# A three-stage kernel (DFT, dense layer, mixture of experts): paced scatters, ScalarE's copies ahead of Gelu, another table of modes, two small products moved

## The chip, the core and the metric

The kernel runs on one core of a Trainium2 chip. The metric is the device time of one execution in microseconds; shown are the median of three runs and one profiled execution. The engines are TensorE (PE; its weight loads are PEld), VectorE (DVE), ScalarE (ACT), GpSimd (POOL) and SyncE (SP, which only starts transfers). Each works through its own queue in order and waits on semaphores of the others.

## What is computed

The reference takes x of 8 batches x 3072 positions x 256 features and does this:

```python
X = np.fft.fft(np.fft.fft(x, axis=1), axis=2).real       # (8, 3072, 256)
x = X.reshape(8 * 3072, 256)
h = x @ w_in                                             # 256 -> 2048
x = (h * (1.0 / (1.0 + np.exp(-1.702 * h)))) @ w_out     # 2048 -> 256
logits = x @ w_gate                                      # 8 experts
expert_idx = np.argmax(logits, axis=1)                   # each expert takes its
# first `capacity` tokens (768), in order of position; for those
out[i] = gate_w[i] * (relu(x[i] @ w1[e]) @ w2[e])        # all others stay 0
```

## The kernel before

The second DFT, over features, is folded into w_in, so the kernel keeps matrices G = DFT x w_in in two parts (a high part in TensorE's 32-bit format and the rest), and the first DFT runs as products of fp16 halves with tables (fft_mm). The symmetry of a real input's transform lets each batch be computed for 1537 rows alone.

The middle part (phase2) goes over 8 batches of 64 units each, 512 units. A batch has four blocks of 384 rows, a block 16 units, one unit per 128 of the 2048 hidden features. In unit u TensorE makes pe, the cosine sum of unit u+1 (m1_even), and po, the sine sum of unit u (m1_odd). E is pe brought out of PSUM. It has two modes, chosen by a table of 64 digits (MODES; the first and last batch have tables of their own): in mode 1 VectorE brings it out and adds a product of two vectors (line 761), in mode 2 TensorE adds that product as a fourth matmul (line 756) and ScalarE copies (line 759). E has three buffers, pe two. VectorE then makes h = E + po and E - po (lines 774, 775), ScalarE the Gelu of h (line 787), and every fourth unit TensorE multiplies the Gelus of four units into acc (line 796), the logits.

Beside these units other work is put in by a timetable: lists pre and post for each unit, worked off ahead of and behind the unit's own operations. It holds, for the next batch, the folds of x on POOL (lines 391 to 408), the scale of that batch (fft_scale: maxima, two small products on TensorE into a tile pss, a few one-column operations on VectorE), the split into fp16 halves, the DFT products, and the preparation of the next block (m1_prep: transpositions psuv, a broadcast psb, u). The tuple SCALE says at which units of a batch the steps of fft_scale run, a negative number meaning ahead of the unit. The tiles pss, psuv, psb and others share one bank of PSUM, so each waits until the one before has been read out.

It also holds the routing of the batch before (route): the logits are transposed, the place of each token in its expert's list is worked out on VectorE, which ends in the addresses ad (line 914), and 24 scatters on POOL (line 920) write 128 rows of 48 bytes each into a table in DRAM, one scatter per unit in the code's order. POOL's queue has no other order than that of the code, and a scatter waits for nothing of its unit. The table is read in the third part (phase3), which gathers each expert's rows, runs the dense layer again for them and then the expert.

Batches count from 0 in the code; the text counts them from the first. The routing of the sixth batch (b = 5 = B - 3) runs within the seventh.

Of the kernel before, what the change touches and what calls it, by code (L numbers as in the profile page):

```python
# [10 lines left out]
F32 = mybir.dt.float32  # L11
# [12 lines left out]
B, S, D = 8, 3072, 256  # L24
# [18 lines left out]
LOADAT = (1, 3, 8)  # L43
NU, CONV, OWN, START1, START = 64, 10, 18, 26, 0
PREP = (5, 8, -9, 10, -11, 12, -13, -14)
SCALE = (-4, 5, -6, 7, -8, 8, 9)
FSTEPS, SSTEPS, SPLIT, SSPAN, SSPAN1 = 20, 9, 13, 11, 10
POINTS = ((16, -11), (25, 5), (29, 13))
SPLIT1, BETWEEN, LAST = 11, 17, (32, 41, 50)
PART = [0, -1, 1, 1, 1, 2, 2, 4, -5, 5, 5, 5, 6, 6, 6, 7, 7, 7, 7, 8, 8, 8, 9, 9, 9]  # L50
ROUTE = [2, -3, 3, -4, 4, -5, 5, 6, 7, 8, 9, 17, -18] + list(range(18, 63))
MODES = [int(c) for c in "1111111212111121122221221111111211111111111111121111111111111121"]
MODES0 = [int(c) for c in "2112111111222122211211221222211212122211222222121112111121112112"]
MODES7 = [int(c) for c in "1111111222212221211222222222112221222122212222222122121212222212"]
ORDER = ((0, 0), (1, 0), (2, 0), (2, 1), (0, 1), (1, 1), (2, 2), (0, 2), (1, 2))
# [126 lines left out]
class K:  # L182
# [561 lines left out]
    def m1_even(self, b, i, f):  # L744
# [4 lines left out]
        x = self.uvt[b, i]  # L749
        mode = (MODES0 if b == 0 else MODES7 if b == B - 1 else MODES)[NFC * i + f]  # L750
        fs = slice(f * P, (f + 1) * P)
# [192 lines left out]
    def timetable(self):  # L944
# [10 lines left out]
        def steps(gen, u0, units):  # L955
            for u in units:
                (pre if u < 0 else post)[u0 + abs(u)].append(gen)
# [28 lines left out]
        for b in range(1, B):  # L986
            s, e = start[b], NU * b
            steps(self.fft_scale(b), s, SCALE)
            s += SPLIT if b > 1 else SPLIT1
# [18 lines left out]
    def route(self, b, parts):  # L1008
        for tiles, t0, nt in parts:
            for a in tiles:  # L1010
                yield from self.route_tiles(b, *a, wait=nt != 15)
                yield
            if b < B - 1:
                del self.lt[b]
            yield from self.route_pos(b, t0, nt)
            for c in range(nt):
                self.route_scatter(b, t0, c)
                yield
            del self.addr[b, t0]
# [8 lines left out]
    def phase2(self):  # L1028
        nc = self.nc
        self.lt, self.info, self.addr = {}, {}, {}  # L1030
        self.hn = 0
        blocks = [(b, i) for b in range(B) for i in range(4)]

        self.parts = [[([(0, 3, 0)], 0, 3)], [([(3, 3, 0)], 3, 3)], [([(6, 3, 0)], 6, 3)],
                      [([(9, 3, 0), (0, 4, 1), (4, 4, 1), (8, 4, 1)], 9, 15)]]
        self.whole = [([(0, 4), (4, 4), (8, 4)], 0, 24)]
        gs, pend, after = {}, [], []
        clears = self.clears()
        hprev, evens = None, []
        accs = {}  # L1040

        def flush_logits():
            j, q, tiles = pend.pop(0)
            b, i = blocks[j]
            if q == 0:
                accs[j] = self.bank("acc", "acc")
            self.m1_logits(b, i, q, tiles, accs[j])
            if q == NFC // 2 - 1:
                after.append((b, i, accs.pop(j)))

        def evac():
            while after:
                b, i, acc = after.pop(0)
                self.m1_evac(b, i, acc)

        def gelu(hp):
            j, f, h = hp
            gs.setdefault((j, f // 2), []).append(self.m1_gelu(*blocks[j], f, h))
            if f % 2 == 1:
                pend.append((j, f // 2, gs.pop((j, f // 2))))  # L1060

        pre, post = self.timetable()

        def take(todo):
            while todo:
                next(todo.pop(0), None)

        for j, (b, i) in enumerate(blocks):
            for f in range(NFC):
                if j == 0:  # L1070
                    next(self.conv, None)
                evac()
                take(pre[NFC * j + f])
                if hprev is not None:
                    gelu(hprev)
                u = NFC * j + f
                while len(evens) < min(1 if u < NFC - 1 else 2, NU * B - u):
                    v = u + len(evens)
                    evens.append(self.m1_even(*blocks[v // NFC], v % NFC))
                hprev = (j, f, self.m1_odd(b, i, f, evens.pop(0)))  # L1080
                if f % LOGITS == 1:
                    while pend:
                        flush_logits()
                if j == 0:
                    next(self.conv, None)
                take(post[NFC * j + f])
                if f == 8 and j >= 4:
                    next(clears, None)
        gelu(hprev)
        while pend:  # L1090
            flush_logits()
        evac()
        self.last_route()
# [213 lines left out]
    def run(self, ctx):  # L1307
        tc, nc = self.tc, self.nc
        ec = ctx.enter_context
        dp = ec(tc.tile_pool(name="dram", bufs=1, space=DRAM))  # L1310
        self.uvflat = dp.tile([B * KH, D], F32, name="uvflat")
        self.uv = self.uvflat.rearrange("(b k) d -> b k d", b=B)
        self.g0 = dp.tile([2, DFF], F32, name="g0")
        self.wo32 = dp.tile([DFF, D], F32, name="wo32")
        self.table = dp.tile([P * self.ncol, 12], I32, name="table")
        banks = ExitStack()
        self.peo = banks.enter_context(tc.tile_pool(name="peo", bufs=1, space=PSUM))
        self.aux = banks.enter_context(ExitStack())
        self.paux = self.aux.enter_context(tc.tile_pool(name="paux", bufs=1, space=PSUM))
        self.banks = {}  # L1320

        cp = ec(tc.tile_pool(name="cp", bufs=1))
        self.acc = cp.tile([P, 8], F32, name="accs")
        self.wog = cp.tile([P, NFC, 32], F32, name="wog")
        nc.gpsimd.memset(self.wog, 0.0)
        self.ones = cp.tile([1, P], F32, name="ones")
        nc.gpsimd.memset(self.ones, 1.0)
        self.selr = cp.tile([P, P], F32R, name="selr")
        self.g3 = cp.tile([P, DFF], F32R, name="g3")
        self.u3, self.ub = {}, {}  # L1330
        self.cf = cp.tile([P, NFC], F32, name="cf")
        self.G = cp.tile([P, 2, 2, DFF], F32R, name="G")
        self.fft_pools = ec(ExitStack())
        fc = self.fft_pools.enter_context
        self.tabp, self.hlp, self.rowp, self.scp, self.fp = [fc(tc.tile_pool(name=n, bufs=1)) for n in ("tabp", "hlp", "rowp", "scp", "fp")]
        self.ctx = ctx

        m1 = ec(ExitStack())
        mc = m1.enter_context
        right = lambda n: tc.tile_pool(name=n, bufs=1, side="right")  # L1340
        lp, self.rp, self.rtp, self.uvp, self.ocp, self.hp = [mc(right(n)) for n in ("lp", "rp", "rtp", "uvp", "ocp", "hp")]
        self.m1p = mc
        self.rt1 = self.rtp.tile([P, D], F32, name="rt1")
        self.start(cp)
        self.iota8 = self.load(lp, "c_iota")
        self.tri = self.load(lp, "c_tri", F16)
        self.infoc = self.load(lp, "c_token", I32)
        self.base = lp.tile([P, E, 1], F32, name="base")
        nc.gpsimd.memset(self.base, 0.0)
        self.smask = {}  # L1350
        for nt in (3, 15, 24):
            self.smask[nt] = lp.tile([P, E, nt + 1], F32, name=f"smask{nt}")
            nc.gpsimd.memset(self.smask[nt], 1.0)
            nc.gpsimd.memset(self.smask[nt][:, :, 0:1], 0.0)
        self.zero = lp.tile([P, D], F32, name="zero")
        nc.gpsimd.memset(self.zero, 0.0)
        tz = self.table.rearrange("(p n) w -> p (n w)", p=P)
        for o in range(0, self.ncol * 12, D):
            w = min(D, self.ncol * 12 - o)
            nc.sync.dma_start(tz[:, o:o + w], self.zero[:, :w].bitcast(I32))  # L1360
        self.phase2()
        m1.close()
        banks.close()
        self.peo = ec(tc.tile_pool(name="p3eo", bufs=4, space=PSUM))
        self.paux = ec(tc.tile_pool(name="p3aux", bufs=4, space=PSUM))
        self.wpool.append(ec(tc.tile_pool(name="wb", bufs=1)))
        self.k3 = ec(tc.tile_pool(name="k3", bufs=1))
        self.tl = self.k3.tile([P, self.ncol, 12], I32, name="tl")
        self.gate = self.k3.tile([P, self.ncol], F32, name="gate")
        self.phase3()  # L1370
# [56 lines left out]
```

## Time and profile before

| | |
|---|---|
| median of three runs | 1942.61 us (1940.83 to 1942.70) |
| profiled execution, its own time | 1941.43 us |
| its span, first to last instruction | 1939.7 us |
| TensorE busy | 1832.8 us (94%) |
| VectorE busy | 1335.6 us (69%) |
| ScalarE busy | 997.7 us (51%) |
| POOL busy | 651.8 us (34%) |
| TensorE's granted clock, mean | 0.981 of full speed |

Busy time is the share in which at least one instruction of the engine was running. Matmuls overlap each other: a row of 0.34 us starts the next after some 0.17 us, so a TensorE that is always busy can still wait a little inside its rows. Idle time before an instruction carries the name of what ended it; "issue" means that the profile shows nothing that the engine waited for, and "remote" that the one who released it is not known.

### The profile page before, as it was taken

What the parts mean: (1) busy time and instruction counts of PE and PEld (TensorE: products, weight loads), DVE (VectorE), ACT (ScalarE), POOL (GpSimd) and SP (SyncE); (2) the same over time, 40 slices, a digit from 0 to 9 for tenths busy, and PEclk for the clock granted to TensorE, in tenths of its full rate; (3) what the DMA queues carried; (4) which work ended last, traced back from release to release, by engine and by line L of the source; (5) the groups of instructions that cost most, each with busy time, mean ns of one, the idle gap of its engine ahead of it and who ended that gap; (6) DMA issues with size and microseconds to landing.
All of it is one profiled execution on the core that took longest, in us unless ns stands there. A gap on an engine that the chain in (4) does not pass through costs nothing.

```text
span 1939.7 us, 34519 instructions
## 1 busy us (share of the span) xinstructions
PE 1832.8 (94%) x12945; PEld 1616.6 (83%) x12945; DVE 1335.6 (69%) x2867; ACT 997.7 (51%) x1798; POOL 651.8 (34%) x779
## 2 busy tenths in 40 slices
PE   3899999999999999995999799999999999999998
PEld 2777777777787777873876499999999999999998
DVE  8978898998989899893888655454545454544442
ACT  4568676766767667672577333332323233333322
POOL 6664639074380844805007431111110011111101
PEclk9899999999999999997999899999999999999999
DMA  7531232232323323220212011010101010111000
GB/s 256 179 105 56 88 106 88 78 109 77 105 88 102 93 67 111 83 69 18 74 49 59 21 49 46 28 50 23 55 12 49 18 50 28 37 34 43 22 9 17
DMA packets 104938, 128.43 MB, mean 66 GB/s; under 512 B 15741, under 2 KB 90517, under 8 KB 104513
## 3 DMA queue, kind: packets, MB, share of 16 engines
q1 hardware_dynamic: 92714, 113.31, 18.2%
q0 software_dynamic: 10752, 12.56, 2.4%
q8 instruction: 102, 1.67, 0.4%
q14 instruction: 66, 0.54, 0.1%
q10 hardware_dynamic: 1304, 0.35, 0.1%
HBM read 77.64 MB, written 47.64 MB: 65 GB/s over the span
## 4 chain that ended last, share of the span: by engine, by line
PE 78%; DVE 11%; issue 4%; ACT 4%; another core or an unknown queue 1%; DMA 1%; POOL 0%; POOLq 0%; ACTq 0%; SPq 0%; DVEq 0%
PE pkh L1194 14%; PE py L1208 14%; PE pe L754 11%; PE po L772 10%; PE acc L796 7%; PE pod L1241 7%; PE pku L1227 7%; PE pf L538 5%; DVE e L761 2%; DVE g L775 1%; DVE h L775 1%; DVE g L774 1%; PE psuv L717 1%; PE pe L756 1%
## 5 line engine op out<-in xcount | busy, mean ns | idle before, releaser
L754 PE MATMUL pe<-uvt,G 128*128 128x384 f32 (+1 forms) x1536 | 389.0, 361 | 24.2 <-ACT e L759 9.7
L787 ACT ACTIVATE g<-g 128x768 f32<-128x768 f32 (+1 forms) x341 | 288.2, 847 | 169.2 <-DVE g L775 156.6
L772 PE MATMUL po<-uvt,G 128*128 128x384 f32 (+1 forms) x1536 | 357.9, 341 | 7.4 <-issue 4.9
L754 PEld LDWEIGHTS pe<-uvt,G 128*128 128x128 f32 x1536 | 256.8, 191 | 73.2 <-DVE e L761 20.8
L1194 PE MATMUL pkh<-kx,G 128*128 128x384 f32 x1536 | 310.3, 339 | 1.5 <-issue 1.3
L1208 PE MATMUL py<-kg,wo 128*128 128x384 f32 x1536 | 307.0, 336 | 1.0 <-issue 1.0
L772 PEld LDWEIGHTS po<-uvt,G 128*128 128x128 f32 x1536 | 275.5, 190 | 15.5 <-issue 5.4
L1251 POOL DMA_INDIRECT out_dram<-ko,tl x48 | 50.4, 1051 | 691.8 <-ACT ko L1250 682.0
L761 DVE SCALAR_TENSOR_TENSOR e<-ub,cf,pe 128x384 f32<-128x384 f32 (+1 forms) x366 | 223.5, 611 | 74.7 <-PE pe L754 37.5
L1208 PEld LDWEIGHTS py<-kg,wo 128*128 128x128 f32 x1536 | 271.5, 188 | 1.7 <-issue 1.7
L1194 PEld LDWEIGHTS pkh<-kx,G 128*128 128x128 f32 x1536 | 263.9, 189 | 3.0 <-issue 2.2
L1197 ACT ACTIVATE kgf<-pkh 128x384 f32<-128x384 f32 x256 | 125.9, 492 | 272.3 <-PE pkh L1194 149.2
L1198 DVE CAST kg<-kgf 128x384 fp32r<-128x384 f32 x256 | 96.4, 376 | 220.5 <-ACT kgf L1197 205.2
L920 POOL DMA_INDIRECT table<-info,ad x192 | 190.2, 991 | 107.2 <-DVE ad L914 60.0
L774 DVE TENSOR_TENSOR g<-e,po 128x384 f32<-128x384 f32 (+1 forms) x341 | 187.8, 551 | 38.0 <-PE po L772 18.7
L787 ACT ACTIVATE h<-h 128x768 f32<-128x768 f32 (+1 forms) x171 | 144.4, 846 | 89.4 <-DVE h L775 83.4
L775 DVE TENSOR_TENSOR g<-e,po 128x384 f32<-128x384 f32 (+1 forms) x341 | 187.4, 550 | 0.0
L1230 DVE SCALAR_TENSOR_TENSOR krl<-pku,krl 128x384 fp32r<-128x384 f32 x128 | 71.4, 558 | 138.3 <-ACT krl L1229 138.3
L1229 ACT ACTIVATE krl<-pku 128x384 fp32r<-128x384 f32 x128 | 63.0, 492 | 197.5 <-PE pku L1227 197.5
L1241 PE MATMUL pod<-w,krl 128*128 128x256 f32 x1152 | 156.5, 280 | 0.0
L1227 PE MATMUL pku<-ky,w 128*128 128x384 f32 x768 | 155.8, 338 | 0.6 <-ACT ky L1215 0.4
L796 PE MATMUL acc<-g,wog 128*32 128x384 f32 (+1 forms) x1364 | 155.0, 492 | 1.2 <-ACT g L787 1.1
(218 smaller groups left out, 2754.6 us busy)
## 6 DMA issues: line engine op xcount, KB each, us to landing
xc<-in_x_dram SPq DMA_DIRECT2D x48, 520.0 KB
out_dram<-zero SPq DMA_DIRECT2D x24, 1024.0 KB
stage<-in_w_dram SPq DMA_DIRECT2D x64, 256.0 KB
rt<-uvflat SPq DMA_DIRECT2D x32, 384.0 KB
f<-in_w_in_dram SPq DMA_DIRECT2D x7, 512.0 KB
f<-in_w_out_dram SPq DMA_DIRECT2D x7, 512.0 KB
uvflat<-ra SPq DMA_DIRECT2D x24, 128.0 KB
table<-info,ad POOLq DMA_INDIRECT x192
```

Of the source, the lines that this page charges most:

```text
L754: nc.tensor.matmul(pe[:, :n2], self.G[:, 0, a, fs], x[:, 0, c, :n2], start=(q == 0), stop=(q == 2 and mode != 2))
L761: nc.vector.scalar_tensor_tensor(e[:, :n], self.ub[b, i][:, :n], self.cf[:, f:f + 1], pe[:, :n], op0=ALU.mult, op1=ALU.add)
L772: nc.tensor.matmul(po[:, :n2], self.G[:, 1, a, fs], x[:, 1, c, :n2], start=(q == 0), stop=(q == 2))
L774: nc.vector.tensor_tensor(h[:, 0, :n], e[:, :n], po[:, :n], op=ALU.add)
L775: nc.vector.tensor_tensor(h[:, 1, :n], e[:, :n], po[:, :n], op=ALU.subtract)
L787: self.nc.scalar.activation(h[:, :, :n], h[:, :, :n], AF.Gelu_apprx_sigmoid)
L796: nc.tensor.matmul(acc[c:c + 32, :n], self.wog[:, 2 * q + j, :], gs[j][:, s, :n], start=(q == 0), stop=(q == NFC // 2 - 1))
L920: ins = nc.gpsimd.indirect_dma_start(out=self.table, out_offset=bass.IndirectOffsetOnAxis(ap=self.addr[b, t0][:, c:c + 1], axis=0), in_=se ...
L1194: nc.tensor.matmul(ps[:, :BS], self.G[:, h, a, fs], x[:, h, c], start=(q == 0), stop=(q == 5))
L1208: nc.tensor.matmul(self.py[n][k][:, :BS], self.wo[:, f, a, k * P:(k + 1) * P], g2[:, c], start=(f == 0 and a == 0 and c == 0), stop=(f == ...
L1227: nc.tensor.matmul(ps[:, :BS], w1[:, k, a, fs], y[:, k, c], start=(q == 0), stop=(q == 5))
L1241: nc.tensor.matmul(ps, r[:, c, t * P:(t + 1) * P], w2[:, F, a, :], start=(F == 0 and c == 0 and a == 0 and t != 1), stop=(F == F2 // P - 1 ...
```

## The change

Four things change. The scatters of the sixth batch's routing each get a copy of one element of E ahead of them on POOL, into a tile pace; self.now is the E that was issued last, which in the timetable's post lists is that of the next unit. In each unit the Gelu of the unit before is issued behind the next unit's pe and E, no more ahead of them. MODES, which holds for the second to the seventh batch, has 19 units of mode 2 in place of 12, every fourth one and three more between. And two steps of fft_scale, the second small product and the maximum that reads it, move by one place.

```diff
-SCALE = (-4, 5, -6, 7, -8, 8, 9)
+SCALE = (-4, 5, -6, 6, -7, 8, 9)
...
-MODES = [int(c) for c in "1111111212111121122221221111111211111111111111121111111111111121"]
+MODES = [int(c) for c in "2111211121112121212121212111211121112111211121112111211121112111"]
...
             for c in range(nt):
+                if b == B - 3:
+                    self.nc.gpsimd.tensor_copy(self.pace, self.now[0:1, 0:1])
                 self.route_scatter(b, t0, c)
                 yield
...
                 take(pre[NFC * j + f])
-                if hprev is not None:
-                    gelu(hprev)
                 u = NFC * j + f
                 while len(evens) < min(1 if u < NFC - 1 else 2, NU * B - u):
                     v = u + len(evens)
                     evens.append(self.m1_even(*blocks[v // NFC], v % NFC))
+                self.now = evens[-1]
+                if hprev is not None:
+                    gelu(hprev)
                 hprev = (j, f, self.m1_odd(b, i, f, evens.pop(0)))
...
+        self.pace = lp.tile([1, 1], F32, name="pace")
```

The order of the instructions at three places. First POOL in the seventh batch, from the memset that ends the DFT of that batch to the next routing; before:

```order
L574 MEMSET r_11596 32x127
L920 DMA table<-info,ad 6144x12 x10
L720 MEMSET uvt 128x2
L920 DMA table<-info,ad 6144x12 x2
L720 MEMSET uvt 128x2
L920 DMA table<-info,ad 6144x12 x12
L829 TENSOR_SCALAR info<-c_token 128x24
```

and now, from the same memset on; the pair of copy and scatter goes on to 24, with the two memsets of uvt between pairs:

```order
L830 TENSOR_SCALAR info<-c_token 128x24
L831 COPY info<-c_token 128x24x2
L574 MEMSET r_11634 32x127
L1018 COPY pace<-e 1x1
L920 DMA table<-info,ad 6144x12
L1018 COPY pace<-e 1x1
```

Each scatter now has a copy of E ahead of it, so none runs before its unit has come that far.

Second ScalarE in an early batch, about units 16 to 21, where the next batch's halves (hi), the logits (lt) and the routing (rk, dt) meet; before:

```order
L874 ACTIVATE dt<-psp 128x8x24
L787 ACTIVATE h<-h 128x2x384
L759 ACTIVATE e<-pe 128x384
L787 ACTIVATE g<-g 128x2x384
L759 ACTIVATE e<-pe 128x384
L479 ACTIVATE hi<-f,sc 128x516
L787 ACTIVATE g<-g 128x2x384
L479 ACTIVATE hi<-f,sc 128x516
L787 ACTIVATE g<-g 128x2x384
L759 ACTIVATE e<-pe 128x384
```

and now:

```order
L874 ACTIVATE dt<-psp 128x8x24
L787 ACTIVATE h<-h 128x2x384
L759 ACTIVATE e<-pe 128x384
L787 ACTIVATE g<-g 128x2x384
L479 ACTIVATE hi<-f,sc 128x516
L787 ACTIVATE g<-g 128x2x384
L479 ACTIVATE hi<-f,sc 128x516
L759 ACTIVATE e<-pe 128x384
L787 ACTIVATE g<-g 128x2x384 x2
```

One E has gone from the stretch, and each E stands one Gelu further ahead: the E of unit u+1 came behind the Gelu of unit u-1 and comes ahead of it now.

Third TensorE at the scale of an early batch, units 5 to 8, from the first small product (pss, line 427) to the transposition psuv; before:

```order
L427 MATMUL pss<-c_ident,sc 1x128
L754 MATMUL pe<-uvt,G 128x384 x3
L756 MATMUL pe<-u_4442,g_78 128x384
L772 MATMUL po<-uvt,G 128x384 x3
L754 MATMUL pe<-uvt,G 128x384 x3
L772 MATMUL po<-uvt,G 128x384 x3
L433 MATMUL pss<-sc,ones 128x1
L754 MATMUL pe<-uvt,G 128x384 x3
L756 MATMUL pe<-u_4442,g_78 128x384
L772 MATMUL po<-uvt,G 128x384 x3
L717 MATMUL psuv<-c_ident,rt 128x128 x3
```

and now:

```order
L427 MATMUL pss<-c_ident,sc 1x128
L754 MATMUL pe<-uvt,G 128x384 x3
L772 MATMUL po<-uvt,G 128x384 x3
L433 MATMUL pss<-sc,ones 128x1
L754 MATMUL pe<-uvt,G 128x384 x3
L756 MATMUL pe<-u_4451,g_78 128x384
L772 MATMUL po<-uvt,G 128x384 x3
L754 MATMUL pe<-uvt,G 128x384 x3
L772 MATMUL po<-uvt,G 128x384 x3
L717 MATMUL psuv<-c_ident,rt 128x128 x3
```

The second product (line 433) stands one unit nearer to the first and one unit further from psuv; of the two matmuls of mode 2 in the stretch one is left.

## Rows read from the trace of the kernel before

**Rows 1.** line 740, two stretches: count, ns, first and last start

```profile
L740 DVE SCALAR_TENSOR_TENSOR u<-psb,c_pick,u3h x5: 596/611/618, 698.6 to 818.3; 128x384 fp32r<-128x384 f32 x4, 128x386 fp32r<-128x386 f32 x1
...
L740 DVE SCALAR_TENSOR_TENSOR u<-psb,c_pick,u3h x5: 596/611/624, 818.3 to 964.7; 128x384 fp32r<-128x384 f32 x4, 128x386 fp32r<-128x386 f32 x1
```

**Rows 2.** us; busy (count) of PE, PEld, DVE, ACT, POOL; PEclk, DMA, GB/s

```profile
698.60:818.30 119.70, 117.55 (x948) 92.34 (x940) 108.72 (x242) 83.31 (x140) 61.34 (x81) 1.00 0.30 92
818.30:964.70 146.40, 122.88 (x948) 95.52 (x940) 108.08 (x242) 77.51 (x125) 27.13 (x39) 0.91 0.17 53
```

**Rows 3.** timeline, POOL: start, us, operation, count [idle <-releaser]

```profile
878.29 1.07 POOL L920 DMA_INDIRECT table<-info,ad  x1 [57.11 <-DVE ad L914]
...
907.74 0.97 POOL L920 DMA_INDIRECT table<-info,ad  x1 [0.30 <-issue]
```

**Rows 4.** timeline, all engines, around the gap

```profile
888.13 0.55 DVE L775 TENSOR_TENSOR g<-e,po 128x384 f32<-128x384 f32 x1
...
896.88 0.48 PE L754 MATMUL pe<-uvt,G 128*128 128x384 f32 x1 [1.62 <-issue]
...
903.92 0.98 ACT L806 ACTIVATE lt<-acc 64x384 f32<-64x384 f32 x2 [17.87 <-remote]
...
912.42 0.61 DVE L761 SCALAR_TENSOR_TENSOR e<-ub,cf,pe 128x384 f32<-128x384 f32 x1 [23.74 <-remote]
...
912.96 0.55 DVE L774 TENSOR_TENSOR g<-e,po 128x384 f32<-128x384 f32 x1
```

**Rows 5.** the scatters of other stretches (line 920), and one matmul in the third

```profile
L920 POOL DMA_INDIRECT table<-info,ad x24: 971/983/1072, 759.9 to 809.6; - x24
...
L920 POOL DMA_INDIRECT table<-info,ad x33: 966/972/1078, 1022.0 to 1084.9; - x33
...
L920 POOL DMA_INDIRECT table<-info,ad x15: 971/972/1318, 1107.2 to 1126.1; - x15
...
1123.77 0.34 PE L1208 MATMUL py<-kg,wo 128*128 128x384 f32 x1 [0.27 <-issue]
```

**Rows 6.** columns of rows 2, four blocks of the fourth batch

```profile
464.30:494.00 29.70, 28.99 (x210) 22.57 (x208) 27.55 (x71) 20.41 (x34) 0.00 (x0) 1.00 0.17 54
494.00:523.80 29.80, 28.49 (x221) 21.67 (x220) 28.12 (x64) 23.41 (x42) 9.64 (x10) 1.00 0.44 139
523.80:553.80 30.00, 30.00 (x261) 24.09 (x260) 26.71 (x57) 19.71 (x32) 26.02 (x34) 1.00 0.34 104
553.80:584.00 30.20, 30.08 (x256) 23.98 (x255) 25.91 (x54) 19.95 (x34) 25.82 (x38) 1.00 0.24 71
```

**Rows 7.** timeline of the same batch, TensorE and ScalarE

```profile
479.47 0.55 PE L717 MATMUL psuv<-c_ident,rt 128*128 128x128 f32 x3 [0.71 <-DVE sc L435]
...
498.31 0.84 ACT L787 ACTIVATE h<-h 128x768 f32<-128x768 f32 x1
499.05 0.49 ACT L759 ACTIVATE e<-pe 128x384 f32<-128x384 f32 x1
...
499.59 0.79 PE L754 MATMUL pe<-uvt,G 128*128 128x384 f32 x3 [1.17 <-ACT e L759]
...
504.19 0.34 PE L756 MATMUL pe<-u,g 128*128 128x384 f32 x1
504.36 0.69 PE L772 MATMUL po<-uvt,G 128*128 128x384 f32 x3
```

**Rows 8.** groups of the whole span: busy us, mean ns | idle before <-releasers

```profile
L754 PE MATMUL pe<-uvt,G 128*128 128x384 f32 (+1 forms) x1536 | 389.0, 361 | 24.2 <-ACT e L759 9.7 <-DVE e L761 8.7 <-issue 5.0
...
L717 PE MATMUL psuv<-c_ident,rt 128*128 128x128 f32 x192 | 31.8, 274 | 5.4 <-DVE sc L435 4.5 <-DVE uvt L723 0.9
...
L717 PEld LDWEIGHTS psuv<-c_ident,rt 128*128 128x128 f32 x192 | 24.2, 140 | 9.9 <-DVE sc L435 6.4 <-DVE uvt L723 1.4 <-DVE G L246 0.2
```

**Rows 9.** timeline, POOL: two of its smallest operations

```profile
890.88 0.11 POOL L720 MEMSET uvt<- 128x2 f32 x1
...
908.78 0.31 POOL L829 TENSOR_SCALAR info<-c_token 128x24 int32<-128x24 int32 x1
```

## The prediction

> **What bounds the kernel now.** I read three things: how long a batch of 64 units takes and what TensorE does in it, then the one batch that is longer, then the small waits that every batch has. VectorE's copy of the next block's sine rows (u, line 740) runs once per block, always at the same place, so four of them are one batch: 119.7 us from 698.6 to 818.3, and 146.4 us from 818.3 to 964.7 [rows 1]. The instruction counts of the two stretches are the same on TensorE and VectorE (948 and 242); TensorE is busy 117.55 of 119.7 us in the first, VectorE 108.72 [rows 2]. So an ordinary batch is bound by TensorE with 2.1 us idle, VectorE is a close second, and the longer batch holds 26.7 us that are nobody's work.
>
> Where they are: POOL begins the 24 scatters of the sixth batch's routing at 878.29, the moment their addresses exist, and fires one each 1.28 us until 907.74 [rows 3]. From 888.13 VectorE starts nothing until 912.42 (23.74 us), ScalarE starts two copies of the logits after 17.87 us of idle time, and TensorE's matmuls come singly, some 0.7 to 2 us apart, released by "issue" [rows 4]. All three are held while POOL alone runs on. The fifth batch's 24 scatters, one batch earlier, lie between POOL's folds, over 49.7 us (2.16 us from one to the next); 33 in the last batch take 62.9 us (1.97 us); those stretches have no such hole. 15 in a burst after the last batch (1.35 us) again bring single matmuls with "issue" before them [rows 5]. So rate decides, not number.
>
> The blocks of an ordinary batch differ [rows 6]: in the third and fourth TensorE is busy 30.00 of 30.00 and 30.08 of 30.20 us, in the first and second 28.99 of 29.70 and 28.49 of 29.80, with VectorE at 27.55 and 28.12. The idle time of the first two has two names: a transposition (psuv) waits 0.71 us for VectorE's small operation on line 435, and a pe matmul waits 1.17 us for ScalarE's copy of E at 499.05, which stood behind a Gelu of 0.84 us [rows 7]. Over the span these are 4.5 and 9.7 us of TensorE idle [rows 8].
>
> **The change part by part.** The sum starts at the profiled execution's 1941.4 us, 1.2 below the median of the runs shown.
>
> *Scatters.* Each of the 24 now stands behind a copy of one element of the E that was issued one unit ahead, so at most one goes per unit: 119.7/64 = 1.87 us on average, between the 1.97 of the last batch, which shows no hole, and the 1.35 of the shorter burst, and far nearer to the former. The sixth batch's routing runs in the seventh batch, where TensorE and VectorE have the work of any other and POOL no folds, so I give that batch the length of its neighbour: 146.4 - 119.7 = 26.7 us less. The copies are new on POOL. Their price lies between 0.11 us (a memset of two columns) and 0.31 us (a 24-column operation) [rows 9]; with 0.97 + 0.30 us for a scatter and its issue a pair takes 1.4 to 1.6 us and fits a unit, so POOL hides it. What queues behind a waiting copy on POOL is the next scatter and two small memsets for uvt; nobody needs the scattered table before the last phase. The copy also reads E, which has three buffers: whoever writes E three units on now waits for POOL, with some 4 us to spare. I take 0 for it. Bounds: 0, and 26.7 kept if the hole stays.
>
> *Scale's small products.* The second matmul of pss goes from the end of unit 7 to the end of unit 6 and line 435 from ahead of unit 8 to ahead of unit 7; the transposition that shares the bank still stands at the end of unit 8. It waited 0.71 us; now a whole unit (1.87 us) lies between. The matmul's own operand, the maximum on VectorE, was queued ahead of unit 6's E and h, and TensorE passes pe and po (1.04 us) before it needs it. Ends: nothing, and the 6.4 us that the weight loads of psuv waited there in six batches [rows 8]. I take 4.0, most of the matmuls' 4.5.
>
> *E ahead of Gelu.* The copy of E no longer waits for a Gelu whose h is made after the same unit's matmuls. It lies ahead of 188 Gelus afterwards, and it waits for pe there, which TensorE finishes before po, so Gelu loses little; Gelu's readers, the logits, come at least one unit later. The 9.7 us are 1.17 in each of six batches and 2.7 in the first and last. Around 499.05 ScalarE's rows have no idle between them [rows 7]; of its E there one falls away by the new table. I take 7.0; ends 0 and 9.7.
>
> *Mode 2.* The table goes from 12 to 19 of 64, in six batches: 42 units more. Each adds one matmul on TensorE, which from its start to the next start takes 504.36 - 504.19 = 0.17 us [rows 7], together 42 x 0.175 = 7.4 us; ScalarE gets 42 x 0.49 us [rows 7] and has room (83.31 of 119.7 us busy); VectorE loses 42 operations that take 912.96 - 912.42 = 0.54 us from start to start [rows 4], 22.7 us. By blocks the count goes 3 to 5, 7 to 6, 1 to 4, 1 to 4. In the third and fourth TensorE has no gap, so their 36 matmuls (6.3 us) are on the path in full; the second gets VectorE work back (28.12 + 0.54 = 28.66 us) and cannot go below that. I take +7.4; the other end is half of it, if VectorE's relief shortens waits under 0.16 us that a row of 0.34 us hides.
>
> Sum: 1941.4 - 26.7 - 4.0 - 7.0 + 7.4 = 1911.1 us. What is late next: TensorE nearly everywhere in these batches, VectorE in the second block.
>
> **The rivals.** (1) *TensorE pays and nothing else comes.* The hole closes, but in the first two blocks VectorE is within 2 us of the block, so the removed waits come back as waits for VectorE, and the matmuls cost their 7.4: 1941.4 - 26.7 + 7.4 = 1922, or 1919 with a part of the waits gone. For it speak 28.12 of 29.80 us; against it, that the two waits had ScalarE and one small product last, not VectorE's stream.
>
> (2) *A price per scatter, not per burst.* If every scatter takes 0.97 us from VectorE wherever it stands, 24 x 0.97 = 23.3 us (the hole is 23.74) stay, spread out: 1911.1 + 23.3 = 1934. Against it: the 119.7 us before hold 24 scatters too, with VectorE busy 108.72 us, and in the hole ScalarE and TensorE stand as well. The Trainium skill, page SBUF — State Buffer, section Who interferes with whom, has such a mechanism: VectorE and GpSimd share a port pair as an exclusive lock, the later one is blocked for a whole instruction, while "PE and ACT never wait on anyone". The trace disagrees here, with ScalarE's 17.87 us and TensorE's single matmuls. By that rule the sum would be the 1934 of this rival.
>
> (3) *The pace is not slow enough.* Units differ in length, scatters bunch behind a short one, and half the hole stays: 1911 + 13 = 1924. The last batch's 33 scatters at a mean of 1.97 us speak against it; that 1.87 is still quicker than any spread-out row speaks for it.
>
> (4) *Slower: POOL holds E.* If a pair of copy and scatter takes longer than a unit, POOL falls behind, E's buffers run out after three units, and both VectorE and ScalarE wait for POOL in 24 units. It decides from 1.87 us per pair; to end above the present time it must cost 30.3 + 3.9 us, 1.4 us in each of 24 units, so 3.3 us per pair: 1946 or more. The rows give 1.4 to 1.6.
>
> (5) *The hole is not the burst's.* It begins only at the ninth scatter; if something else in that stretch makes it, pacing leaves it whole: 1941.4 - 4.0 - 7.0 + 7.4 = 1937.8, no change that can be told. Against it: the same signs at the burst of 15, and at no other place.
>
> **How the numbers follow.** Forecast 71%, rival 1 15%, rival 2 5%, rival 3 4%, rival 5 3%, rival 4 2%. The likeliest gives 1911 us. Best end of the known bounds: 1941.4 - 26.7 - 6.4 - 9.7 + 3.7 = 1902. The range goes from there to 1926, over rivals 1 and 3. What a measurement of this kernel can tell from no change is about 0.2%, 3.9 us. The forecast and rivals 1 to 3 are faster by more, rival 5 lies within it, rival 4 is slower: 95, 3 and 2.
>
> **What would show it.** The hole: four u copies of the seventh batch 119 to 121 us apart, scatters there 1.5 to 3 us apart, no wait of VectorE over 2 us. Scale: no idle of psuv behind line 435. E: the pe matmuls' idle for line 759 under 3 us. Mode 2: 188 of line 756, the third and fourth block 0.3 to 0.5 us longer, the second not shorter than 28.7. Wrong would be: VectorE or ScalarE waiting for POOL at E (rival 4), E operations stretched or late by about 1 us at each scatter (rival 2), a hole that begins a few scatters later (rival 3), or blocks one and two unchanged (rival 1).

## The result and the profile after

The changed kernel takes 1917.48 us (median of five runs, 1913.82 to 1919.78), against 1942.61 before: a ratio of 0.987, 95% interval 0.9859 to 0.9881, 25.1 us less. Its profiled execution took 1919.8 us with a span of 1917.7, so it is one of the longer of the five.

The u copies of line 740 and the stretches between them, as in [rows 1] and [rows 2] (a stretch's columns: us; busy and count of PE, PEld, DVE, ACT, POOL; granted clock; DMA share; GB/s), the sixth batch first, then the seventh:

```profile
L740 DVE SCALAR_TENSOR_TENSOR u<-psb,c_pick,u3h x5: 595/614/614, 699.9 to 820.5; 128x384 fp32r<-128x384 f32 x4, 128x386 fp32r<-128x386 f32 x1
...
L740 DVE SCALAR_TENSOR_TENSOR u<-psb,c_pick,u3h x5: 596/614/615, 820.5 to 940.8; 128x384 fp32r<-128x384 f32 x4, 128x386 fp32r<-128x386 f32 x1
...
699.94:820.49 120.55, 119.37 (x951) 94.00 (x948) 105.57 (x236) 85.16 (x145) 61.48 (x81) 1.00 0.29 91
820.49:940.84 120.35, 119.17 (x951) 93.91 (x948) 105.22 (x236) 79.75 (x131) 30.09 (x59) 1.00 0.21 65
```

The seventh batch fell from 146.4 to 120.35 us and is now like its neighbour, with a granted clock of 1.00 where 0.91 stood. But the neighbour grew, from 119.7 to 120.55. POOL's timeline in the seventh batch (start, us, operation, count, idle before), against [rows 3]:

```profile
883.26 0.17 POOL L1018 COPY pace<-e 1x1 f32<-1x1 f32 x1
883.68 0.97 POOL L920 DMA_INDIRECT table<-info,ad  x1 [0.25 <-issue]
884.66 0.18 POOL L1018 COPY pace<-e 1x1 f32<-1x1 f32 x1
885.18 0.98 POOL L920 DMA_INDIRECT table<-info,ad  x1 [0.35 <-issue]
...
886.69 0.97 POOL L920 DMA_INDIRECT table<-info,ad  x1 [0.35 <-issue]
889.07 0.18 POOL L1018 COPY pace<-e 1x1 f32<-1x1 f32 x1 [1.41 <-DVE e L761]
889.81 0.98 POOL L920 DMA_INDIRECT table<-info,ad  x1 [0.56 <-issue]
```

The copy does wait for E. Where E is there already, a scatter follows the one before after 1.3 to 1.5 us; where it isn't, after up to 3.3 us. All 24 lie between 882.2 and 924.8 us, 1.85 us apart on average. The groups of the whole span that answer to [rows 8], with po and the mode-2 matmuls beside them:

```profile
L754 PE MATMUL pe<-uvt,G 128*128 128x384 f32 (+1 forms) x1536 | 382.7, 357 | 3.3 <-ACT e L759 2.8
L772 PE MATMUL po<-uvt,G 128*128 128x384 f32 (+1 forms) x1536 | 356.7, 340 | 7.8 <-DVE g L775 4.1 <-DVE h L775 1.6 <-issue 0.2
L756 PE MATMUL pe<-u,g 128*128 128x384 f32 (+1 forms) x188 | 63.8, 339 | 0.2 <-DVE u L740 0.2
L717 PE MATMUL psuv<-c_ident,rt 128*128 128x128 f32 x192 | 31.4, 272 | 1.2 <-DVE uvt L723 1.2
```

Both named waits went: pe behind ScalarE's E from 9.7 to 2.8 us, psuv behind line 435 from 4.5 to none. In their place po now waits behind VectorE's line 775, 4.1 and 1.6 us. The blocks of the fourth batch, against [rows 6]:

```profile
463.20:493.10 29.90, 29.68 (x216) 23.18 (x218) 27.28 (x68) 20.54 (x36) 0.00 (x0) 1.00 0.16 53
493.10:522.50 29.40, 28.44 (x219) 21.69 (x220) 28.14 (x64) 23.22 (x41) 10.01 (x11) 1.00 0.47 143
522.50:554.20 31.70, 31.70 (x267) 25.37 (x265) 25.69 (x55) 20.87 (x36) 27.19 (x35) 1.00 0.31 96
554.20:583.80 29.60, 29.60 (x255) 23.83 (x254) 24.35 (x51) 20.67 (x35) 24.46 (x36) 1.00 0.24 73
```

The third and fourth together went from 60.2 to 61.3 us; the second lost 0.4, the first gained 0.2 although its wait of 0.71 us is gone: TensorE's busy time there rose from 28.99 to 29.68.

For all kernels below, the profiled execution is cut at the first h of a batch (line 774) and, for the last two columns, at the end of the last h, in us; "before" is the median that the kernel before had on the same chip.

| kernel | before | batch 1 | 2 to 6 | 7 | 8 | after the last unit |
|---|---|---|---|---|---|---|
| before | 1942.6 | 140.8 | 599.3 | 146.4 | 118.2 | 851.5 |
| after | 1942.6 | 137.5 | 603.1 | 120.3 | 118.1 | 854.3 |
| e1, pacing alone | 1939.2 | 139.1 | 598.3 | 119.2 | 117.9 | 850.4 |
| e2, after without pacing | 1939.2 | 137.4 | 601.5 | 147.4 | 117.8 | 850.0 |
| e3, after with old MODES | 1939.2 | 135.4 | 594.4 | 118.6 | 117.8 | 852.8 |
| e4, pacing and E | 1939.2 | 135.3 | 594.9 | 118.7 | 117.8 | 850.8 |
| e5, bursts of 8 | 1908.6 | 136.7 | 592.4 | 117.9 | 117.8 | 848.6 |
| e6, bursts of 12 | 1908.6 | 134.8 | 592.5 | 117.8 | 117.8 | 848.5 |
| e7, memset ahead of each | 1908.6 | 135.3 | 592.9 | 118.0 | 118.1 | 848.9 |
| e8, after with old SCALE | 1908.6 | 134.7 | 598.6 | 119.7 | 117.8 | 848.5 |
| e9, bursts of 12 again | 1907.9 | 136.6 | 592.6 | 117.8 | 117.8 | 848.7 |
| e10, memset again | 1907.9 | 136.2 | 593.0 | 118.0 | 118.1 | 848.7 |
| e11, pause in the last phase | 1907.9 | 135.3 | 592.4 | 117.9 | 117.8 | 851.8 |
| e12, 12 spaced, 12 in a burst | 1939.0 | 137.7 | 596.1 | 127.2 | 117.8 | 854.6 |

### The profile page after: what moved, and what is told of

It is laid out like the page before. It is cut to its first block, busy times and chain, and to the rows that moved or that the text cites. A ratio compares the mean times of both kernels' runs of the same rounds, so it can differ in the third digit from the quotient of the medians.

```text
span 1917.7 us, 34590 instructions
## 1 busy us (share of the span) xinstructions
PE 1840.2 (96%) x12987; PEld 1626.4 (85%) x12987; DVE 1316.5 (69%) x2825; ACT 1008.4 (53%) x1840; POOL 656.3 (34%) x803
## 4 chain that ended last, share of the span: by engine, by line
PE 83%; DVE 11%; issue 4%; DMA 1%; ACT 1%; POOL 0%; POOLq 0%; SPq 0%; DVEq 0%; ACTq 0%
PE pkh L1197 14%; PE py L1211 14%; PE pe L754 12%; PE po L772 11%; PE acc L796 8%; PE pod L1244 7%; PE pku L1230 7%; PE pf L538 5%; DVE g L775 1%; DVE e L761 1%; PE pe L756 1%; DVE g L774 1%; DVE lo L481 1%; DVE h L775 1%; PE psuv L717 1%
## 5 line engine op out<-in xcount | busy, mean ns | idle before, releaser
L754 PE MATMUL pe<-uvt,G 128*128 128x384 f32 (+1 forms) x1536 | 382.7, 357 | 3.3 <-ACT e L759 2.8
L761 DVE SCALAR_TENSOR_TENSOR e<-ub,cf,pe 128x384 f32<-128x384 f32 (+1 forms) x324 | 197.3, 609 | 56.0 <-PE pe L754 39.4
```

Of the source, the lines that this page charges most:

```text
L754: nc.tensor.matmul(pe[:, :n2], self.G[:, 0, a, fs], x[:, 0, c, :n2], start=(q == 0), stop=(q == 2 and mode != 2))
L761: nc.vector.scalar_tensor_tensor(e[:, :n], self.ub[b, i][:, :n], self.cf[:, f:f + 1], pe[:, :n], op0=ALU.mult, op1=ALU.add)
```

## The four edits, taken apart

**Pacing alone.** The kernel before with the copies ahead of the scatters, E's and Gelu's order, MODES and SCALE as they were.

```diff
             for c in range(nt):
+                if b == B - 3:
+                    self.nc.gpsimd.tensor_copy(self.pace, self.now[0:1, 0:1])
                 self.route_scatter(b, t0, c)
...
+                self.now = evens[-1]
...
+        self.pace = lp.tile([1, 1], F32, name="pace")
```

> The kernel before with the paced scatters alone; order of Gelu and E, MODES and SCALE as before. Theory A (the hole is made by the burst of scatters, and is all that pacing changes): 1942.6 - 26.7 = 1916, the seventh batch 119 to 121 us, and the phase after the last batch as before. Theory B (the hole is not the burst's, and the other edits closed it): 1942.6, hole whole. Theory C (each scatter has a price, now spread out): a seventh batch of over 125 us, 1922 or more.

Measured: 1911.8 us against 1939.16, ratio 0.9857 (0.9841 to 0.9874), 27.4 us less; the seventh batch 119.2. Theory A.

**All but pacing.** The same lines taken out of the changed kernel.

> The changed kernel without the copies that pace the scatters; the other three edits stay. Theory A (burst makes the hole): the hole is back, 1917.5 + 26.7 = 1944, so that the three other edits together give nothing or cost 1 to 2 us. Theory B (the other edits closed the hole): 1917. If the three other edits gain what the prediction gave them (3.6 us): 1939.

Measured: 1941.52 us, ratio 1.001 (1.0002 to 1.0019), the seventh batch 147.4. Two stretches of its hole:

```profile
884.00:898.00 14.00, 5.40 (x30) 2.93 (x27) 2.65 (x5) 0.85 (x1) 10.87 (x14) 0.62 0.02 1
898.00:911.00 13.00, 3.08 (x6) 1.44 (x5) 0.00 (x0) 0.97 (x2) 8.19 (x11) 0.50 0.02 1
```

The hole is back whole, with other orders of E, other modes and another scale around it. The three other edits together give nothing (by the medians they cost 2.4 us); the prediction had a gain of 3.6 us for them. Which one failed, the runs below say.

**The old table of modes.**

```diff
-MODES = [int(c) for c in "2111211121112121212121212111211121112111211121112111211121112111"]
+MODES = [int(c) for c in "1111111212111121122221221111111211111111111111121111111111111121"]
```

> The changed kernel with the table MODES of before (12 units of mode 2 in place of 19). Theory A (the 42 added matmuls are on TensorE's path at 0.175 us each, and the removed waits are real gains): 1917.5 - 7.4 = 1910, third and fourth block back at 60.2 us together. Theory D (in a saturated TensorE the removed waits come back as waits for VectorE, and mode 2 was what relieved VectorE): 1917 to 1920, with more idle of po for VectorE than in the changed kernel. Theory E (the new order of E and Gelu costs, by the new waits of po for VectorE's g): 1917.

Measured: 1906.43 us, ratio 0.9828 (0.9815 to 0.9841). The changed kernel's 0.987 is 0.0042 or 8.1 us above, against 7.4 for the 42 matmuls; batches 2 to 6 are 7.1 us shorter than those of e2, which has the new table on the same chip (35 x 0.175 = 6.1). Theory A as to the matmuls: mode 2 gave nothing back for its price. Whether both removed waits were gains, this run doesn't tell.

**E ahead of Gelu, no other edit but pacing.** The kernel with pacing alone, and Gelu behind E as in the change.

```diff
                 take(pre[NFC * j + f])
-                if hprev is not None:
-                    gelu(hprev)
...
                 self.now = evens[-1]
+                if hprev is not None:
+                    gelu(hprev)
```

> The kernel before with the paced scatters and the copy of E ahead of Gelu; MODES and SCALE as before. Theory A (E's 9.7 us of idle are gains): 7 us under the pace-only kernel, so 1909, with the idle of pe behind ScalarE's E under 3 us. Theory D (the waits come back as waits for VectorE): 1914 to 1917. Theory E (the order costs): 1918 or more.

Measured: 1904.02 us, ratio 0.9818 (0.9806 to 0.9831), 7.8 us under the kernel with pacing alone. Unit 18 of the fourth batch, where ScalarE's E had been late, without this edit and with it:

```profile
498.50:500.72 2.22, 1.13 (x7) 0.81 (x5) 1.59 (x3) 2.20 (x7) 0.00 (x0) 1.00 0.21 45
```

```profile
490.29:491.71 1.42, 1.23 (x8) 0.91 (x6) 1.42 (x4) 1.41 (x5) 0.00 (x0) 1.00 0.22 47
```

TensorE was idle 1.09 us of 2.22 here, and VectorE 0.63; ScalarE alone had no gap. When E came earlier, the unit shrank by 0.80 us, until VectorE had no gap either (1.42 of 1.42). The unit is 0.8 us shorter in each of batches 2 to 6; these five lose 3.4 us in all, and the first batch, where E was late in three places, 3.8.

This kernel differs from e3 by SCALE alone, and is not slower but 2.4 us faster. The three units at the scale, without the edit (e4) and with it (e3):

```profile
469.08:470.81 1.73, 1.73 (x11) 1.47 (x10) 1.73 (x5) 1.31 (x2) 0.00 (x0) 1.00 1.11 391
470.81:472.34 1.53, 0.95 (x6) 0.63 (x4) 1.53 (x6) 1.15 (x3) 0.00 (x0) 1.00 0.39 129
472.34:474.95 2.61, 2.48 (x21) 1.69 (x25) 2.54 (x11) 1.65 (x3) 0.00 (x0) 1.00 0.02 4
```

```profile
469.85:471.64 1.79, 1.79 (x11) 1.77 (x12) 1.79 (x5) 1.37 (x2) 0.00 (x0) 1.00 1.09 387
471.64:473.11 1.47, 1.47 (x12) 1.43 (x11) 1.47 (x4) 1.02 (x3) 0.00 (x0) 1.00 0.38 129
473.11:475.73 2.62, 2.62 (x23) 1.36 (x22) 2.55 (x10) 1.71 (x3) 0.00 (x0) 1.00 0.01 3
```

Without the edit TensorE idles 0.58 us in the second unit; with it none. The three units take 5.87 and 5.88 us. In each, the third number in front of a bracket, VectorE's, is the unit's whole length, but for 0.07 us. The wait that was removed was that of an engine which was ahead of VectorE, and it came back inside TensorE's rows. The 2.4 us of the medians lie elsewhere: by the table, 2.0 us of the difference stand after the last unit, where no edit works. So with the old table of modes the edit of SCALE gives nothing.

**The changed kernel with the old SCALE.**

```diff
-SCALE = (-4, 5, -6, 6, -7, 8, 9)
+SCALE = (-4, 5, -6, 7, -8, 8, 9)
```

> The changed kernel with SCALE as before: paced scatters, E ahead of Gelu, the new MODES. Theory V (VectorE has no idle time in units 6 to 17 of a batch, so that the removed wait of psuv bought nothing): the time of the changed kernel, 0.987 of before, within 0.001. If the edit gains the 4.0 us of the prediction: 0.989. If it costs, as the difference of 2.4 us between the two kernels with the old MODES hints: 0.9855 to 0.986.

Measured: 1907.1 us against 1908.58, ratio 0.9992 (0.9983 to 1.0001). It fits none of the three, because of the chip: there the kernel before takes 1908.6 us, as if it had no hole. Against its neighbours on that chip (e5 to e7, 1898.9 to 1899.7, which have the old MODES and the old SCALE) it is 7.4 to 8.2 us slower, the price of the 42 matmuls once more. What it says of the whole change: without a hole to close, pacing, E and the modes come to nothing.

It also says what the edit of SCALE does in the changed kernel. The same three units, 6 to 8 of the fourth batch, in the changed kernel and then in e8:

```profile
475.09:476.84 1.75, 1.75 (x11) 1.74 (x12) 1.35 (x5) 0.54 (x2) 0.00 (x0) 1.00 1.07 374
476.84:478.83 1.99, 1.99 (x14) 1.95 (x13) 1.99 (x4) 1.57 (x3) 0.00 (x0) 1.00 0.32 114
478.83:481.45 2.62, 2.62 (x24) 1.36 (x23) 2.55 (x10) 1.20 (x2) 0.00 (x0) 1.00 0.01 4
```

```profile
471.82:473.03 1.21, 1.21 (x8) 0.96 (x6) 1.21 (x4) 0.53 (x2) 0.00 (x0) 1.00 1.08 377
473.03:475.10 2.07, 1.92 (x12) 1.58 (x13) 2.07 (x7) 1.59 (x2) 0.00 (x0) 1.00 0.60 208
475.10:477.70 2.60, 2.60 (x25) 1.34 (x23) 2.53 (x9) 1.34 (x2) 0.00 (x0) 1.00 0.02 7
```

They take 6.36 us with the edit and 5.88 without it, and all six batches from the second to the seventh show such a difference. The two kernels ran on different chips, but that is not the chip: e2, on the chip of e3 and e4, has the new MODES and the new SCALE and takes 6.35, while e3 and e4 take 5.88 and 5.87 there, and e5 takes 5.87 on the chip of e8. With the new table VectorE has a gap in unit 6, busy 1.35 of 1.75 us, and the first operation of unit 7 ends it:

```profile
476.84 0.56 DVE L774 TENSOR_TENSOR h<-e,po 128x384 f32<-128x384 f32 x1 [0.40 <-PE po L772]
```

TensorE starts that po some 0.5 us later after the unit's begin than in e8 (at 476.10, 1.01 us in, against 472.30, 0.48 us in), since the small product that was moved now stands ahead of pe and po. So neither edit alone lengthens these units, and the two together cost 0.48 us in each of six batches, 2.9 us. Theory V's time can't be compared on this chip, and its reason holds for the old table alone.

## The burst, and the chips

All kernels from here on are e4 with something else ahead of the scatters. First, bursts with pauses and a distance without waiting:

```diff
-                if b == B - 3:
+                if b == B - 3 and c % 8 == 0:
```

(12 in place of 8 for the next), and for the third

```diff
-                    self.nc.gpsimd.tensor_copy(self.pace, self.now[0:1, 0:1])
+                    self.nc.gpsimd.memset(self.pace, 0.0)
...
-        self.pace = lp.tile([1, 1], F32, name="pace")
+        self.pace = lp.tile([1, 512], F32, name="pace")
```

> The kernel with paced scatters and E ahead of Gelu (0.9818 of the time of before, seventh batch 118.7 us), with the pacing copy only ahead of every eighth scatter: three bursts of 8 at 1.28 us with pauses of some 5 us. Theory P (TensorE is starved once it has issued some 65 to 85 matmuls since a burst began; in this part that takes 7 to 8 us): the last one or two scatters of each burst starve it, seventh batch 120 to 124 us. Theory N (the number of scatters that lie in one unbroken burst decides, more than 12 being harmful): no starving, 118.7 us. Theory M (the mean rate over some 45 us decides): 118.7 us too.

> As the kernel with bursts of eight, with the copy ahead of every twelfth scatter: two bursts of 12 at 1.28 us, 15.4 us long. Theory P (starved after 65 to 85 matmuls of a burst, 7 to 8 us): the last 5 scatters of each starve it, about 6 us lost twice, seventh batch 129 to 132 us. Theory N (more than 12 in a burst being harmful): 118.7 us. Theory M (the mean rate decides): 118.7 us.

> As the kernel with paced scatters and E ahead of Gelu, but each scatter stands behind a memset of 512 columns of POOL's own, 0.55 us by the rows of such memsets, instead of a copy that waits for E: a burst of 24 pairs, some 1.85 us each, that waits for nothing of the units. Theory R (the distance of the scatters decides, whatever makes it): seventh batch 118 to 120 us and 0.981 to 0.983 of the time of before. Theory W (the wait for each unit is what helps, since POOL then never runs ahead): the hole is there, 135 us or more for that batch.

Measured: 1899.72, 1898.86 and 1899.67 us, ratios 0.9955, 0.9949 and 0.9958 (intervals of 0.0015 to either side), the seventh batch 117.8 to 118.0. They told nothing of the theories, since the kernel before took 1908.58 us on that chip: 30.6 us less than on the chip of the runs above. The first burst of 12 there, the scatters and two stretches:

```profile
L920 POOL DMA_INDIRECT table<-info,ad x12: 968/972/1075, 869.4 to 883.6; - x12
...
869.40:877.20 7.80, 7.80 (x72) 6.37 (x72) 6.62 (x15) 5.53 (x9) 5.95 (x7) 1.00 0.24 71
877.20:884.60 7.40, 7.40 (x63) 5.83 (x62) 7.25 (x17) 3.69 (x5) 5.99 (x8) 1.00 0.25 77
```

Twelve scatters at 1.29 us, and TensorE busy 7.40 of 7.40 us to their end, VectorE 7.25. By the rule of the Trainium skill that the prediction named as its second rival (page SBUF — State Buffer, section Who interferes with whom), a VectorE instruction with at most one input from SBUF, outside the two-port modes, does not contend with GpSimd. Lines 774 and 775 take E from SBUF and po from PSUM, so by the rule they lose nothing to the scatters, and these rows agree. The prediction left that condition out when it put 1934 us down to the rule.

The same two kernels once more, on another chip, and with them a pause in the last phase, whose 15 scatters come in a burst of their own:

```diff
+        gap = self.k3.tile([1, 512], F32, name="gap")
         for c in range(15):
+            for _ in range(3 if c == 8 else 0):
+                self.nc.gpsimd.memset(gap, 0.0)
             self.route_scatter(B - 1, LAST0, c)
```

> The kernel with two bursts of 12 again (E ahead of Gelu, pacing copy ahead of every twelfth scatter). On a chip where the kernel before takes 1939 us or more: theory P (TensorE starved after 65 to 85 matmuls of a burst) wants a seventh batch of 129 to 132 us; theories N and M (more than 12 in a burst, or the mean rate over 45 us) want 118 to 119 us. On a chip where the kernel before takes 1908 to 1909 us no burst starves TensorE, and it is 0.995 of before with 118 us, as in the run ahead of this one; that decides nothing but says again that the chip is what differs.

> The kernel with a memset of 0.55 us ahead of each of the 24 scatters and no wait for E, again (1.65 us from scatter to scatter on the chip of the run ahead of this one). On a chip where the kernel before takes 1939 us or more: theory R (distance decides) wants a seventh batch of 118 to 119 us and 0.981 to 0.983 of before; theory W (the wait for the units is what helps) wants 130 us or more. On a chip without the hole: 0.996 of before, nothing decided.

> Paced scatters and E ahead of Gelu, and in the last phase three memsets (some 1.7 us) ahead of the ninth of the 15 scatters. Theory P: TensorE counts from the pause, so the 15 scatters no longer starve it at their end; after the last unit 849 us are left, in place of 850 to 854 on chips with the hole, and the table comes 1.7 us later, which nobody waits for. Theory N (more than 12 in a burst): the same, 849. If a pause of 1.7 us doesn't matter: 850 to 854, TensorE's starts falling from 11 or 12 to 3 to 7 in 2 us at the end of the 15 scatters. On a chip without the hole: 848.5, no difference.

Measured: again a chip without the hole (before 1907.9 us): 0.9948, 0.9955 and 0.9959. The pause was not free: in its profiled execution 851.8 us after the last unit against 848.7 of its two neighbours. Four stretches of it where the second gather's rows are transposed:

```profile
1090.00:1095.00 5.00, 5.00 (x30) 5.00 (x29) 2.98 (x7) 2.27 (x3) 2.04 (x2) 1.00 0.61 189
1095.00:1098.00 3.00, 0.99 (x5) 0.32 (x3) 1.53 (x5) 2.30 (x3) 2.09 (x4) 1.00 0.31 90
1098.00:1102.00 4.00, 3.89 (x14) 3.79 (x15) 2.50 (x6) 0.98 (x2) 1.94 (x2) 0.57 0.33 98
1102.00:1108.00 6.00, 6.00 (x37) 6.00 (x36) 2.40 (x5) 1.74 (x4) 0.00 (x0) 1.00 0.01 3
```

The table that came 1.7 us later made TensorE idle 2.0 us at 1095 (two of the transpositions waited 1.03 and 0.90 us for the gathered rows), and behind that the granted clock was 0.57 for 4 us. The expectation that nobody waits there was wrong.

The last run puts both distances into one batch: 12 scatters behind a memset of 512 columns each, then 12 in a burst.

```diff
-                if b == B - 3:
-                    self.nc.gpsimd.tensor_copy(self.pace, self.now[0:1, 0:1])
+                if b == B - 3 and c < 12:
+                    self.nc.gpsimd.memset(self.pace, 0.0)
```

> E ahead of Gelu as before, and in the seventh batch 12 scatters each behind a memset of POOL's own (1.65 us from one to the next, no wait for a unit), then 12 in one burst at 1.28 us. On a chip where the kernel before takes 1939 us or more: theory R (distance decides) wants TensorE at full pace through the first 12, theory W (only a wait for the units helps) wants it starved there too; theory P (starved after 65 to 85 matmuls of a burst) wants some 6 us lost in the second 12, a seventh batch of 124 to 126 us, theory N (more than 12 in a burst) 118 to 119 us there. On a chip where before takes 1908 us: 118 us, 0.995 of before, and what starves TensorE on the other chips stays open between P, N, R and W.

Measured, on a chip where before takes 1939.03: 1916.51 us, ratio 0.9882 (0.9866 to 0.9899), the seventh batch 127.2, 8.5 us over that of e4. The two groups of scatters, and the stretches through them:

```profile
L920 POOL DMA_INDIRECT table<-info,ad x12: 967/972/1075, 871.7 to 890.0; - x12
...
L920 POOL DMA_INDIRECT table<-info,ad x12: 971/972/981, 891.3 to 905.3; - x12
...
871.70:891.30 19.60, 19.60 (x167) 16.40 (x167) 17.26 (x37) 11.85 (x18) 17.55 (x26) 1.00 0.30 95
891.30:898.00 6.70, 6.70 (x60) 5.24 (x59) 3.75 (x8) 3.31 (x5) 5.18 (x6) 1.00 0.04 4
898.00:906.00 8.00, 3.64 (x17) 1.89 (x19) 1.63 (x3) 0.85 (x1) 6.17 (x7) 0.82 0.03 1
906.00:912.00 6.00, 5.73 (x32) 3.31 (x25) 3.71 (x9) 2.10 (x4) 0.99 (x4) 0.67 0.07 24
```

Twelve scatters 1.66 us apart leave TensorE busy 19.60 of 19.60 us. The next twelve, 1.27 us apart, leave it alone for 6.7 us, and then it has 3.64 of 8.00. Theory R holds and W falls: no wait for a unit is needed. N falls: twelve in a row are enough, here behind twelve spaced ones. M falls: all 24 lie within 45 us here (871.7 to 905.3) as in the changed kernel, which has no hole. P's onset and its loss of some 6 us come near (7 us, 8.5 us), but its reason does not fit. VectorE stops first, behind an operation of 896.20, and TensorE, which went on to 898.5, then waits for VectorE's E:

```profile
901.17 0.61 DVE L761 SCALAR_TENSOR_TENSOR e<-ub,cf,pe 128x384 f32<-128x384 f32 x1 [4.42 <-remote]
901.84 0.79 PE L754 MATMUL pe<-uvt,G 128*128 128x384 f32 x3 [3.32 <-DVE e L761]
```

So a count of TensorE's matmuls is not what stops this batch. What does stays open. Two candidates can be set aside. The DMA engines are not full: their share was 0.02 in the hole of e2 above. Nor does a late transfer of instructions end the hole: in the trace of before none starts between 885 and 925 us, while the engines resume at 912.

The last phase has a burst of 15 in every kernel, and shows the same difference of chips. A stretch within it, its end and what follows on the chip of e12, then its end on the chip of e9:

```profile
1090.00:1096.00 6.00, 6.00 (x36) 6.00 (x35) 1.84 (x4) 0.83 (x2) 4.78 (x5) 1.00 0.02 1
1097.00:1103.00 6.00, 2.69 (x10) 1.71 (x9) 0.72 (x2) 0.00 (x0) 3.24 (x4) 0.84 0.02 1
1103.00:1108.00 5.00, 5.00 (x18) 4.90 (x17) 3.41 (x8) 1.85 (x4) 1.82 (x2) 0.51 0.62 181
```

```profile
1082.00:1088.00 6.00, 6.00 (x37) 6.00 (x35) 3.00 (x6) 1.48 (x3) 4.24 (x4) 1.00 0.02 1
```

Ten matmuls in 6 us and a granted clock of 0.51 behind them, against 37 in 6 us at 1.00. After the last unit the kernels take 848.5 to 848.9 us on the chips without starving (e11's pause aside) and 850.0 to 854.6 on the others.

## Why the prediction came near, and where it missed

It said 1911 us, 30.3 less than its own execution; 1917.5 came, 25.1 less by the medians. That lies nearer to rival 1's 1919 than to the forecast, but not for rival 1's reason alone: one of the two waits paid, the other edit cost. Term by term, with what the runs gave:

| term | predicted | measured | from |
|---|---|---|---|
| hole | -26.7 | -27.4 | e1 |
| E ahead of Gelu | -7.0 | -7.8 | e4 against e1 |
| scale's small products | -4.0 | +2.9 | after against e8, 6 x 0.48 (with the old MODES 0: e3 5.88, e4 5.87 us) |
| mode 2 | +7.4 | +7.4 to +8.2 | e8 against e5 to e7 |
| last phase | 0 | +2.8 | 854.3 against 851.5 |

The measured column, with 7.7 for mode 2, comes to -21.8. The two profiled executions, from which the last term is taken, differ by 21.65 us (1941.43 and 1919.78); the medians differ by 25.1, since the profiled execution of before was 1.2 us under its median and that of after 2.3 over.

**The hole.** Right in size and place, and the runs bear out its reading of [rows 5] that number alone does not decide: 24 scatters are harmless when spread, 12 in a row are not. A short run is harmless too, since in the changed kernel two or three follow each other at 1.3 us. What no profile of one chip could tell is that the hole belongs to some chips only. Rival 5 is out (e2 has the hole with all other edits), rival 2 too (e1 has all 24 scatters and a seventh batch of 119.2 us), rival 3 as well (the scatters do bunch in the changed kernel, and the batch has no hole).

**Scale's small products: the step that failed.** "It waited 0.71 us; now a whole unit lies between" is true of the wait, which is gone, and false of the time. The prediction had the sign against it in hand, VectorE's 27.55 of 29.70 us in the first block [rows 6], and rival 1 said what then happens; it was set aside because the waits "had ScalarE and one small product last, not VectorE's stream". Line 435 is itself in VectorE's stream, behind unit 7's h and the routing's operations, and this stream has no gap from unit 6 to unit 8. VectorE's 2 idle us lie elsewhere in the block. That is why the edit gave nothing with the old table. In the changed kernel it cost 0.48 us a batch: the moved product delays pe and po in unit 6, VectorE waits 0.40 us there for po, and the wait it was to remove was down to 0.15 us (psuv behind line 435 in e8, fourth batch). The prediction priced the edit by the wait alone and gave TensorE's new order no price; that the two edits act on each other it did not consider. For this wait rival 1 was right, for E's it was wrong.

**E.** The size is right and its parts are not: 0.7 us per batch in place of 1.17, since VectorE becomes the limit in that unit after 0.80, and 3.8 in the first batch, of which a part may be chance: e5 and e6, the same code there, differ by 1.9, of which 1.6 lie in four units at the scale (10.80 and 9.16 us) that took 10.55 in e1 and 9.18 in e4.

**Mode 2.** Right: the price of 42 matmuls, in full. The relief for VectorE, 1335.6 to 1316.5 us, bought nothing that the time of the kernel shows.

**Last phase.** Not in the sum. Against the 848.5 us of the chips without the hole, the profiled execution of before took 3.0 us more there and that of after 5.8; by e12's rows it is the end of the burst of 15 that takes them. No edit is near it; on such chips it lay anywhere from 850.0 to 854.6.

**The signs.** The u copies are 120.4 us apart over a batch, psuv doesn't wait for line 435, pe waits 2.8 us for line 759, line 756 stands 188 times, the third and fourth block together are 1.1 us longer (0.6 to 1.0 was said), the second has 29.4. One sign came out wrong: no wait of VectorE over 2 us was said, and one of 2.4 us for POOL stands at line 761 in the seventh batch; ScalarE's E waits 1.9 us for a pacing copy there. That is rival 4's mechanism in small. The batch is no longer than its neighbour, so no cost of these waits shows.

## What to carry to other kernels

A wait is worth its length only where no other engine is busy through it: cut windows of one unit, not of a block, and look whether the next engine has a gap there. Unit 18 had one (VectorE 1.59 of 2.22) and paid 0.80 us; unit 7 had none (1.53 of 1.53) and paid nothing. An instruction that is moved can also delay what now stands behind it: with the other table of modes the same edit cost 0.48 us a batch. Scatters are better spread than fired in a row, which on the chip of e12 took an operation of half a microsecond between them and no wait; and of a change's parts, measure each alone: pacing and E without the other two take 0.9818 of before (1904.0 us), the change as it stands 0.987.

## What the runs showed of the hardware

Chips differ: the same kernel before takes 1937 to 1944 us where e1 to e4, e12 and the changed kernel ran, and 1907 to 1911 us on the two chips of e5 to e11. By its time before has no such hole there; it was not profiled there. Of the 30.6 us between the two kinds, the hole is 27.4 (e1); for the rest, kernels differ between the two kinds after the last unit (850.0 to 854.6 us against 848.5) and in batches 2 to 6, where the same code takes 594.9 us in e4 and 592.4 in e5. On the first kind, 24 scatters in a row, 1.27 to 1.28 us apart, cost 27.4 us, 12 in a row 8.5, and 12 at 1.66 us nothing; it sets in some 7 us into a burst in the seventh batch. On the second kind, bursts of 12 and 15 show nothing. What the chips do differently isn't shown.

Such a hole costs more than its idle time. In [rows 2] the longer batch is 26.7 us longer, but TensorE's idle time grew by 21.4 us alone; the other 5.3 us are busy time of the same number of matmuls. TensorE's granted clock was 0.50 (the 1.2 GHz level) from 898 to 911 us in e2, where it was busy 3.08 of 13 us, and 0.51 for 5 us of full work in the last phase of e12; after e11's idle time of 2.0 us it was 0.57 over the next 4.
